# Unpacking 64-bit weights with three bit operations in place of four on VectorE

## The chip, the cores and the metric

The kernel runs on one core of a Trainium2 chip. The metric is the device time of one execution in microseconds. A core has five engines that run side by side, each its own queue in order: TensorE (PE in the profile; PEld is its weight load), VectorE (DVE), ScalarE (ACT), GpSimd (POOL) and SyncE (SP), which here only issues DMAs. They wait for each other by semaphores.

## The reference

Attention with a window and with global tokens (8 batches, 8 heads, 512 local and 32 global tokens, head size 64), and behind it a feed-forward block over the 8 x 544 tokens:

```python
s_ll = scale * np.matmul(q_l, k_l.transpose(0, 1, 3, 2))
mask = np.abs(pos[:, None] - pos[None, :]) <= window
...
x = np.ascontiguousarray(attn_out.transpose(0, 2, 1, 3)).reshape(B * S, H * D)
...
h = x @ w_in
g = np.maximum(h, 0.0) + np.log1p(np.exp(-np.abs(h)))
return (g @ w_out).astype(np.float32)
```

The two weights (512 x 2048 and 2048 x 512) come as 64-bit floats, all else as 32-bit floats.

## The kernel before

**Feed-forward.** Each product is formed from three matmuls in TensorE's rounded 32-bit format: a value is split into a rounded high part and the rest, and high by high, high by rest and rest by high are added. `hpart` makes h for 128 hidden units (f, sixteen of them) and 512 tokens of a batch (b), `act` makes g of it (ScalarE: L529 to L531 and the rounding L535; VectorE: L532, which also frees the bank of h; GpSimd: the rest, L536), `opart` adds g times w_out up. h has two banks, so the third h waits for the first L532. `split_x` and, for the first heads, `split0` split the attention's output into xh (ScalarE) and xl (VectorE, L225).

**Attention.** The first eight heads (four pairs, m below 4) go through a pipeline of steps in `local` and `glob`: `scores0`, maximum and exponentials (`soft0`, L164 to L167), weighing on GpSimd (L179), transposes, products with v. The other head pairs go in pieces: `scores` into s_ps (L306 copies them to SBUF on ScalarE, L311 takes maxima into mt), `maxima` folds them (L324 to L337), `probs` lays them out again with VectorE transposes (L345, tile mb, two buffers), subtracts on GpSimd (L350 to L353), takes exponentials (L354) and sums (L359, tile zt); `totals` inverts the sums; `values` and `normalise` make the output (v_ps, L394 to L399). All pieces of later batches lie among the feed-forward products of the batch before.

**The weights.** A weight tile (kind wi or wo, number k from 0 to 15) is 128 x 512 64-bit floats, which `load_w` brings to SBUF as pairs of 32-bit words, low and high. It becomes 32-bit floats in four bit steps and is then split:

- `abs_w` (L468, ScalarE): absolute value of the high word, read as a 32-bit float, into the tile wbits.
- `bits_w` (VectorE): L475 raises it to at least 2^-15, so that the exponent can't fall out of range; L477 shifts it left by 3 and masks the upper two bits off; L478 puts the high word's upper two bits back in; L481 puts the low word's upper three bits in at the bottom. The result is the 32-bit float, written over the low word.
- `halves_w`: L486 rounds it (ScalarE), L487 takes the rest (GpSimd).

The tiles go in the order of `order_w`: wi0 to wi3, wo0, wo1, wi4, wi5, wo2, wo3, wi6, wi7 and so on. Eleven or twelve of them are handled in the steps of the first heads, one a step, with VectorE's and ScalarE's order there written out by `keep` and `note`; the rest (`weights`) beside batch 0 of the feed-forward block.

**The order.** TensorE's order is written out: `mm` chains every matmul to the one before. On VectorE, ScalarE and GpSimd a list scheduler with a timeline of its own sets the order outside the chained steps, from its own costs of the instructions; so a change of one instruction can move others.

Of the kernel before, what the change touches and what calls it, by code (L numbers as in the profile page):

```python
# [8 lines left out]
F32 = mybir.dt.float32  # L9
# [3 lines left out]
AF = mybir.ActivationFunctionType  # L13
ALU = mybir.AluOpType
# [28 lines left out]
SPACE = 3  # L43
AHEAD = 4

TINY = 2.0 ** -15


def windows(ap2d, start, stride, count, width):
# [5 lines left out]
def moe_over_global_local_attention(  # L55
# [11 lines left out]
    nc = tc.nc  # L67
# [51 lines left out]
    def after(i, what):  # L119

        if what in order:
            tc.add_manual_dep(i.ins, order[what].name, mybir.DependencyInfo(mybir.DependencyClass.NoSync, mybir.DependencyReason.DATA), reason="order")
        return i
# [26 lines left out]
    def keep(what, i):  # L150
        order[what] = after(i, what).ins
# [292 lines left out]
    wi, wo, raws = {}, {}, {}  # L444
# [13 lines left out]
    def note(what, i):  # L458
        if tight:
            keep(what, i)  # L460
        return i

    def abs_w(kind, k):
        if A_LO <= k < NF - A_UP:
            a = pl.tile([P, 512], I32, tag=f"{kind}{k + A_UP}", name=f"wbits{kind}{k}", bufs=1)
        else:
            a = pl.tile([P, 512], I32, tag="mb", name=f"wbits{kind}{k}", bufs=2)
        note("act", nc.scalar.activation(a.bitcast(F32), raws[kind, k][:, :, 1].bitcast(F32), AF.Abs))  # L468
        return a

    def bits_w(kind, k, a):
        t = raws.pop((kind, k))
        lo32, hi32 = t[:, :, 0], t[:, :, 1]

        i = nc.vector.tensor_scalar(a.bitcast(F32), a.bitcast(F32), TINY, None, op0=ALU.max)  # L475
        note("dve", i) if tight else after(i, "maxima")
        note("dve", nc.vector.tensor_scalar(a, a, 3, 0x3FFFFFFF, op0=ALU.logical_shift_left, op1=ALU.bitwise_and))  # L477
        note("dve", nc.vector.scalar_tensor_tensor(a, hi32, -0x40000000, a, op0=ALU.bitwise_and, op1=ALU.bitwise_or))  # L478

        r = lo32 if k < NF - 1 else pl.tile([P, 512], I32, tag="mb", name=f"wlast{kind}", bufs=2)  # L480
        note("dve", nc.vector.scalar_tensor_tensor(r, lo32, 29, a, op0=ALU.logical_shift_right, op1=ALU.bitwise_or))  # L481
        return r.bitcast(F32)
# [6 lines left out]
    def split_w(kind, k):  # L489
        halves_w(kind, k, bits_w(kind, k, abs_w(kind, k)))  # L490
# [104 lines left out]
    i = order_w.index(("wi", NF - 1))  # L595
# [39 lines left out]
    for k in range(-2, n + 2):  # L635
        stage(k + 2, 0)

        while k >= n - 2 and pcs[0][0] < min(12 * M0 + 8 * (k - n + 3), START):
            pcs.pop(0)[1]()
        if k == 0:  # L640
            key_masks()
        if held:
            r = bits_w(*held)
        stage(k + 2, 1)
        stage(k - 2, 5)
        stage(k - 2, 6)
        stage(k, 3)
        stage(k, 4)
        stage(k + 2, 2)
        if held:  # L650
            halves_w(*held[:2], r)
            held = None
        if -1 <= k and wk[1] < W_PRE:
            held = order_w[wk[1]]
            held += (abs_w(*held),)
            wk[1] += 1
    tight = False
    if held:
        halves_w(*held[:2], bits_w(*held))
# [74 lines left out]
```

## Time and profile before

| | us |
|---|---|
| median of three runs | 1016.42 (1015.89 to 1018.9) |
| profiled execution | 1018.0 |
| its span, first to last instruction | 1016.2 |
| TensorE busy | 963.4 |
| VectorE busy | 676.4 |
| ScalarE busy | 512.6 |
| GpSimd busy | 451.7 |

The profile is of one execution. In a line of the 40 slices each digit is the busy share in tenths of a slice of 25 us; PEclk is the clock that TensorE was granted. In a group of instructions stand line, engine, operation, output and inputs with shapes, count, then busy time in all, mean time of one in ns, and the engine's idle time just before them. In a timeline a row has start and length in us. Neighbouring instructions of one engine overlap by some hundredths of a microsecond.

### The profile page before, as it was taken

The page shows a single profiled execution, that of the slowest core. Times are in us where ns is not written, and L with a number is a line of the kernel's source. Part 1 is how long each engine was busy: PE and PEld are TensorE (multiplying, and loading weights), DVE is VectorE, ACT ScalarE, POOL GpSimd, SP SyncE. Part 2 cuts the span into 40 slices and gives each one's busy share as a digit, 9 for nine tenths or more (in the row PEclk, how much of TensorE's full clock was granted, in tenths as well). Part 3 has the DMA queues.
Part 4 walks back from the last instruction along what each step waited for, and adds up shares of the span by engine and source line. Part 5 has one row for each costly group of instructions (what it writes and reads, how often), then busy time and mean ns, then how long its engine had stood idle before and what let it go on. Part 6 is the DMA issues. An engine that isn't in the chain of part 4 may idle for free.

```text
span 1016.2 us, 14213 instructions
## 1 busy us (share of the span) xinstructions
PE 963.4 (95%) x5098; PEld 750.6 (74%) x5098; DVE 676.4 (67%) x1428; ACT 512.6 (50%) x882; POOL 451.7 (44%) x614
## 2 busy tenths in 40 slices
PE   6685988999999999999999999999999999999996
PEld 4553666777777777777777777777777777888895
DVE  6879989797667767776678766776677665211210
ACT  5754655555444544554445544554455445544452
POOL 4645675654444544344444544444435444222221
PEclk9897988999999999999999999999999999999998
DMA  9540441121111211121112111121112100100000
GB/s 353 206 146 19 167 140 57 51 70 53 44 48 48 85 42 46 35 88 48 39 48 89 48 42 43 57 80 44 41 47 76 46 17 1 63 0 1 22 22 21
DMA packets 34607, 65.94 MB, mean 65 GB/s; under 512 B 7656, under 2 KB 11752, under 8 KB 34536
## 3 DMA queue, kind: packets, MB, share of 16 engines
q1 hardware_dynamic: 33992, 64.96, 20.0%
q8 instruction: 40, 0.66, 0.3%
q14 instruction: 31, 0.25, 0.1%
q10 hardware_dynamic: 544, 0.07, 0.0%
HBM read 55.57 MB, written 9.44 MB: 64 GB/s over the span
## 4 chain that ended last, share of the span: by engine, by line
PE 81%; DVE 9%; POOL 3%; issue 3%; ACT 2%; DMA 1%; SPq 0%; POOLq 0%; ACTq 0%; DVEq 0%
PE o L126 35%; PE h L126 34%; PE s_ps L126 6%; PE v_ps L126 5%; POOL s L350 1%; DVE wbitswi L478 1%; DMA woraw<-in_w_out 1%; DVE wiraw L481 1%; DVE sums L164 1%; DVE wbitswo L478 1%; DVE wbitswi L475 1%; POOL gl L536 1%; ACT e L167 1%; POOL wo L487 1%; DVE wbitswo L475 0%
## 5 line engine op out<-in xcount | busy, mean ns | idle before, releaser
L126 PE MATMUL h<-xh,wi 128*128 128x512 f32 (+1 forms) x1152 | 351.7, 389 | 18.6 <-DVE xl L225 12.7
L126 PE MATMUL o<-wo,gh 128*128 128x512 f32 x1088 | 347.2, 400 | 0.0
L536 POOL TENSOR_TENSOR gl<-e,gh 128x512 fp32r<-128x512 f32 x136 | 178.6, 1314 | 328.0 <-ACT gh L535 258.2
L126 PEld LDWEIGHTS h<-xh,wi 128*128 128x128 f32 x1152 | 210.2, 190 | 68.5 <-issue 18.2
L126 PEld LDWEIGHTS o<-wo,gh 128*128 128x128 f32 x1088 | 200.6, 189 | 51.3 <-ACT e L529 3.8
L532 DVE SCALAR_TENSOR_TENSOR e<-h,e 128x512 f32<-128x512 f32 x136 | 93.1, 685 | 218.1 <-ACT e L531 197.2
L126 PE MATMUL h<-xl,wi 128*128 128x512 f32 (+1 forms) x576 | 220.8, 383 | 0.0
L126 PE MATMUL o<-wo,gl 128*128 128x512 f32 x544 | 214.6, 395 | 0.0
L529 ACT ACTIVATE e<-h 128x512 f32<-128x512 f32 x136 | 81.1, 597 | 224.6 <-PE h L126 224.4
L535 ACT CAST gh<-e 128x512 fp32r<-128x512 f32 x136 | 84.3, 620 | 121.3 <-DVE e L532 121.2
L350 POOL TENSOR_TENSOR s<-s,mb 128x384 f32<-128x384 f32 x112 | 114.2, 1049 | 57.4 <-DVE mb L345 57.3
L126 PEld LDWEIGHTS h<-xl,wi 128*128 128x128 f32 x576 | 109.2, 190 | 22.6
L126 PEld LDWEIGHTS o<-wo,gl 128*128 128x128 f32 x544 | 102.7, 189 | 24.0 <-POOL gl L536 0.2
L531 ACT ACTIVATE e<-e,one 128x512 f32<-128x512 f32 x136 | 98.4, 723 | 4.2
L354 ACT ACTIVATE s<-s 128x768 f32<-128x768 f32 (+1 forms) x84 | 66.4, 790 | 47.2 <-POOL s L350 41.7
L530 ACT ACTIVATE e<-e 128x512 f32<-128x512 f32 x136 | 85.7, 630 | 3.3
L310 DVE TENSOR_TENSOR s<-s_ps,mask 128x768 f32<-128x768 f32 (+1 forms) x96 | 64.6, 694 | 29.3 <-PE s_ps L126 29.3
L126 PE MATMUL s_ps<-raw 64*128 64x192 f32 (+1 forms) x672 | 79.0, 348 | 4.5 <-issue 4.5
L126 PEld LDWEIGHTS s_ps<-raw 64*128 64x128 f32 x672 | 53.5, 189 | 36.2 <-issue 28.7
L359 DVE TRANSPOSE_TENSOR_REDUCE zt<-s 128x24 f32<-128x768 f32 (+1 forms) x84 | 75.3, 901 | 6.7 <-ACT s L354 4.5
L311 DVE TRANSPOSE_TENSOR_REDUCE mt<-s 128x24 f32<-128x768 f32 (+1 forms) x84 | 74.6, 888 | 3.6 <-ACT s L306 2.9
L126 PE MATMUL v_ps<-s,v 128*64 128x192 f32 (+1 forms) x672 | 58.1, 324 | 3.9 <-ACT s L306 3.2
(129 smaller groups left out, 852.7 us busy)
## 6 DMA issues: line engine op xcount, KB each, us to landing
raw<-in_qk SPq DMA_DIRECT2D x56, 272.0 KB, 2.7
v<-in_v SPq DMA_DIRECT2D x28, 384.0 KB, 3.0
out<-ot SPq DMA_DIRECT2D x34, 256.0 KB, 2.2
wiraw<-in_w_in SPq DMA_DIRECT2D x16, 512.0 KB, 8.5
woraw<-in_w_out SPq DMA_DIRECT2D x16, 512.0 KB, 7.1
raw<-in_qk SPq DMA_DIRECT2D x28, 224.0 KB, 2.5
v<-in_v SPq DMA_DIRECT2D x4, 512.0 KB, 9.1
raw<-in_qk SPq DMA_DIRECT2D x4, 416.0 KB, 7.4
```

The costliest lines, as they stand in the source:

```text
L126: order["pe"] = after(nc.tensor.matmul(*a, **k), "pe").ins
L310: nc.vector.tensor_tensor(s[:, :, o:o + w], ps[:, :, o:o + w], mk.unsqueeze(1).to_broadcast([P, 2, w]), op=ALU.add)
L311: order["scores"] = nc.vector.tensor_reduce(windows(mt, 3 + 12 * p, 36, 2, nb), s.rearrange("p h (b k) -> p h b k", k=32), axis=AX.X, op=A ...
L350: nc.gpsimd.tensor_tensor(sw, sw, windows(mb[:, h], 0, 96, 2, 192), op=ALU.subtract)
L354: nc.scalar.activation(s, s, AF.Exp, scale=0.125)
L359: nc.vector.tensor_reduce(windows(st["zt", m], 3 + 12 * p, 36, 2, nb), s.rearrange("p h (b k) -> p h b k", k=32), axis=AX.X, op=ALU.add, a ...
L529: nc.scalar.activation(e, ph, AF.Abs)
L530: nc.scalar.activation(e, e, AF.Exp, scale=-1.0)
L531: nc.scalar.activation(e, e, AF.Ln, bias=one)
L532: nc.vector.scalar_tensor_tensor(e, ph, 0.0, e, op0=ALU.max, op1=ALU.add)
L535: nc.scalar.copy(gh, e)
L536: nc.gpsimd.tensor_tensor(gl, e, gh.bitcast(F32), op=ALU.subtract)
```

## The change

```diff
-TINY = 2.0 ** -15
+DROP = 2.0 ** -112
+SIGN = -0x80000000
...
     def abs_w(kind, k):
...
-        note("act", nc.scalar.activation(a.bitcast(F32), raws[kind, k][:, :, 1].bitcast(F32), AF.Abs))
+        note("act", nc.scalar.activation(a.bitcast(F32), raws[kind, k][:, :, 1].bitcast(F32), AF.Copy, scale=DROP))
...
     def bits_w(kind, k, a):
...
-        i = nc.vector.tensor_scalar(a.bitcast(F32), a.bitcast(F32), TINY, None, op0=ALU.max)
+        i = nc.vector.tensor_scalar(a, a, 3, None, op0=ALU.logical_shift_left)
         note("dve", i) if tight else after(i, "maxima")
-        note("dve", nc.vector.tensor_scalar(a, a, 3, 0x3FFFFFFF, op0=ALU.logical_shift_left, op1=ALU.bitwise_and))
-        note("dve", nc.vector.scalar_tensor_tensor(a, hi32, -0x40000000, a, op0=ALU.bitwise_and, op1=ALU.bitwise_or))
+        note("dve", nc.vector.scalar_tensor_tensor(a, hi32, SIGN, a, op0=ALU.bitwise_and, op1=ALU.bitwise_or))
```

ScalarE now multiplies the high word, read as a 32-bit float, by 2^-112. That takes 112 off its exponent field, which holds the upper eight of the 64-bit float's eleven exponent bits, and 112 times 8 is 896, the difference between the two formats' offsets. What is left of the exponent fits below the top when it is shifted left by 3 (new L476), so nothing has to be masked; values too small come out as zero without the maximum. The shift drops the sign, which the merge (new L478) takes from the high word. Per tile VectorE has three instructions (L476, L478, L481) in place of four. The constant's new line moves the line numbers up to L476 by one; from L480 on they are the same.

TensorE has the same instructions in the same order. On VectorE, ScalarE and GpSimd the scheduler moves others, too. Three places matter below. In each the buffer's number is the last part of a name.

VectorE, where the first pair's maxima (mt4) have been folded and head pair 4's transposes (mb4) follow; L311 (new L312) is the reduction of head pair 5's scores. Before:

```order
L337 COPY mt4_656<-mt4_656 32x42 x3
L311 TENSOR_REDUCE mt5_768<-s5_1_816 128x2x12
L345 STREAM_TRANSPOSE mb4_0_739<-mt4_656 128x576
L345 STREAM_TRANSPOSE mb4_1_747<-mt4_656 128x576
L311 TENSOR_REDUCE mt5_768<-s5_2_845 128x2x9
```

and changed:

```order
L338 COPY mt4_648<-mt4_648 32x42 x3
L346 STREAM_TRANSPOSE mb4_0_730<-mt4_648 128x576
L346 STREAM_TRANSPOSE mb4_1_738<-mt4_648 128x576
L312 TENSOR_REDUCE mt5_759<-s5_1_806 128x2x12
L312 TENSOR_REDUCE mt5_759<-s5_2_835 128x2x9
```

The two transposes now stand ahead of the reduction.

VectorE, up to the last xl of the first heads (L225, new L226), the last input of the first feed-forward product. Before:

```order
L337 COPY mt5_768<-mt5_768 32x42 x3
L475 TENSOR_SCALAR wbitswi8_1056<-wbitswi8_1056 128x512
L475 TENSOR_SCALAR wbitswi9_1094<-wbitswi9_1094 128x512
L478 SCALAR_TENSOR_TENSOR wbitswi6_805<-wiraw6_158,wbitswi6_805 128x512
L359 TENSOR_REDUCE zt4_744<-s4_2_723 128x2x9
L345 STREAM_TRANSPOSE mb5_0_861<-mt5_768 128x576
L477 TENSOR_SCALAR wbitswi8_1056<-wbitswi8_1056 128x512
L477 TENSOR_SCALAR wbitswi9_1094<-wbitswi9_1094 128x512
L481 SCALAR_TENSOR_TENSOR wiraw6_158<-wiraw6_158,wbitswi6_805 128x512
L225 TENSOR_TENSOR xl0_3_789<-o0_3_1_885,xh0_3_788 128x256
```

and changed:

```order
L478 SCALAR_TENSOR_TENSOR wbitswi6_795<-wiraw6_158,wbitswi6_795 128x512
L338 COPY mt5_759<-mt5_759 32x42 x3
L476 TENSOR_SCALAR wbitswi8_1042<-wbitswi8_1042 128x512
L476 TENSOR_SCALAR wbitswi9_1079<-wbitswi9_1079 128x512
L360 TENSOR_REDUCE zt4_735<-s4_2_714 128x2x9
L481 SCALAR_TENSOR_TENSOR wiraw6_158<-wiraw6_158,wbitswi6_795 128x512
L226 TENSOR_TENSOR xl0_3_779<-o0_3_1_874,xh0_3_778 128x256
L346 STREAM_TRANSPOSE mb5_0_851<-mt5_759 128x576
```

The shifts of wi8 and wi9 are gone, the transpose of head pair 5 (mb5) stands behind xl, and the first merge of wi6 has moved ahead of the copies. On GpSimd the rest of wi6 (L487) now stands ahead of head pair 5's subtractions, behind the first of which it stood.

ScalarE, where head pair 7's last scores are copied from PSUM (L306, new L307), which frees the bank for the next v_ps. Before:

```order
L486 CAST wo12_1561<-woraw12_1429 128x512
L306 COPY s7_2_1624<-s_ps7_2_1615 128x576
L535 CAST gh0_9_1590<-e0_9_1585 128x512
L486 CAST wo13_1600<-woraw13_1455 128x512
```

and changed:

```order
L486 CAST wo12_1533<-woraw12_1406 128x512
L530 ACTIVATE e0_9_1557<-e0_9_1557 128x512
L531 ACTIVATE e0_9_1557<-e0_9_1557,one_102 128x512
L486 CAST wo13_1571<-woraw13_1431 128x512
L535 CAST gh0_9_1562<-e0_9_1557 128x512
L307 COPY s7_2_1595<-s_ps7_2_1586 128x576
```

The copy now stands behind the rounding of wo13 and of the ninth tile of g (gh0_9), and so behind what VectorE does for them.

## The prediction

> **What bounds the kernel now.** I read the page first, for which engine sets the end and from when on.
>
> ```profile
> span 1016.2 us, 14213 instructions
> PE 963.4 (95%) x5098; PEld 750.6 (74%) x5098; DVE 676.4 (67%) x1428; ACT 512.6 (50%) x882; POOL 451.7 (44%) x614
> PE   6685988999999999999999999999999999999996
> DVE  6879989797667767776678766776677665211210
> PEclk9897988999999999999999999999999999999998
> PE 81%; DVE 9%; POOL 3%; issue 3%; ACT 2%; DMA 1%; SPq 0%; POOLq 0%; ACTq 0%; DVEq 0%
> ```
>
> TensorE (PE) is full except in the first slices of 25 us, where VectorE (DVE) is. The weights are unpacked only there. The stages of the busy-time table make it sharp (in each row: stretch, its length, then busy time of PE, PEld, DVE, ACT, POOL, then the granted clock).
>
> ```profile
> core 0: us, PE busy (x) PEld busy (x) DVE busy (x) ACT busy (x) POOL busy (x), PEclk, DMA share, GB/s
> 14.00:44.00 30.00, 19.63 (x185) 14.83 (x183) 28.93 (x55) 23.28 (x70) 17.73 (x28) 1.00 0.85 327
> 71.00:85.00 14.00, 1.31 (x7) 1.04 (x6) 11.94 (x26) 5.46 (x9) 9.87 (x16) 0.64 0.31 117
> 98.00:110.00 12.00, 12.00 (x51) 8.74 (x52) 11.91 (x24) 7.71 (x13) 9.20 (x6) 0.86 0.45 157
> 110.00:130.00 20.00, 17.84 (x87) 12.78 (x86) 18.14 (x24) 13.28 (x24) 11.69 (x10) 1.00 0.46 162
> 130.00:150.00 20.00, 16.90 (x81) 12.40 (x80) 18.44 (x36) 11.62 (x19) 14.29 (x17) 0.83 0.39 135
> 150.00:170.00 20.00, 18.53 (x92) 13.69 (x90) 19.60 (x32) 10.39 (x18) 11.97 (x10) 1.00 0.09 25
> 170.00:190.00 20.00, 18.71 (x88) 14.52 (x89) 17.18 (x36) 12.14 (x20) 15.61 (x19) 0.83 0.19 63
> 235.00:1000.00 765.00, 765.00 (x4000) 603.45 (x3999) 474.22 (x1033) 373.39 (x601) 316.29 (x435) 1.00 0.15 45
> ```
>
> From 235 us TensorE is busy 765.00 of 765 us at full clock: nothing done on VectorE there can shorten or lengthen the end. Since the order on TensorE is the same in the changed program, the end comes earlier by just as much as TensorE gets through its first 216 us earlier. From 98 to 190 us VectorE is busy 85.3 of 92 us (the five rows summed), while TensorE waits now and then. Its eight longest waits from its first feed-forward product on, from TensorE's timeline (start, length, and in brackets the idle time before it and what ended it):
>
> ```profile
> 84.30 1.19 PE L126 MATMUL h<-xh,wi 128*128 128x512 f32 x2 [12.69 <-DVE xl L225]
> 97.98 0.74 PE L126 MATMUL h<-xh,wi 128*128 128x512 f32 x2 [3.07 <-DVE e L532]
> 114.93 0.73 PE L126 MATMUL h<-xh,wi 128*128 128x512 f32 x2 [0.89 <-DVE e L532]
> 122.03 0.73 PE L126 MATMUL h<-xh,wi 128*128 128x512 f32 x2 [1.27 <-DVE e L532]
> 140.14 1.01 PE L126 MATMUL s_ps<-raw 64*128 64x192 f32 x4 [2.67 <-issue]
> 171.29 3.79 PE L126 MATMUL v_ps<-s,v 128*64 128x192 f32 x24 [2.76 <-ACT s L306]
> 206.39 2.01 PE L126 MATMUL v_ps<-s,v 128*64 128x192 f32 x24 [0.68 <-DVE s L310]
> 214.61 1.47 PE L126 MATMUL s_ps<-raw 64*128 64x192 f32 x8 [1.82 <-issue]
> ```
>
> The sum is 25.85 us, half of it in the first. That is the room.
>
> **The change, part by part.** Per weight tile (32 of them) one VectorE instruction goes. The maximum (old L475) becomes a shift on the same tile, the old shift-with-mask (L477) is gone, and both merges stay.
>
> ```profile
> L477 DVE TENSOR_SCALAR wbitswo<-wbitswo 128x512 int32<-128x512 int32 x16 | 11.6, 730 | 0.3
> L477 DVE TENSOR_SCALAR wbitswi<-wbitswi 128x512 int32<-128x512 int32 x16 | 9.6, 602 | 0.2
> L475 DVE TENSOR_SCALAR wbitswi<-wbitswi x16: 378/424/1512, 15.4 to 185.8; 128x512 f32<-128x512 f32 x16
> L477 DVE TENSOR_SCALAR wbitswo<-wbitswo x16: 407/428/1547, 35.4 to 203.6; 128x512 int32<-128x512 int32 x16
> ```
>
> The new shift is an integer instruction of one operation, of which the trace has none; its neighbours, the float maximum (median 424 ns) and the integer shift-with-mask (428), cost the same, so I count the swap as nothing. The removed one costs 0.43 us by its median, 0.66 by its mean (21.2 us over 32), at least 0.38 (the maximum's least). Median and mean differ by waits for GpSimd (POOL), as one step of the first loop shows:
>
> ```profile
> 20.16 0.55 DVE L477 TENSOR_SCALAR wbitswi<-wbitswi 128x512 int32<-128x512 int32 x1
> 20.40 1.46 POOL L487 TENSOR_TENSOR wi<-wiraw,wi 128x512 fp32r<-128x512 f32 x1
> 20.74 1.66 DVE L478 SCALAR_TENSOR_TENSOR wbitswi<-wiraw,wbitswi 128x512 int32<-128x512 int32 x1
> 23.80 0.66 ACT L468 ACTIVATE wbitswi<-wiraw 128x512 f32<-128x512 f32 x1
> 24.56 0.62 DVE L475 TENSOR_SCALAR wbitswi<-wbitswi 128x512 f32<-128x512 f32 x1
> ```
>
> The merge L478 ends at 22.40, half a microsecond after GpSimd's subtraction ended at 21.86, and took 1.66. Had the shift not stood ahead of it, it or the next merge would have met that subtraction all the same. So I take 0.43, with 0.66 as the upper end. The Trainium skill's page "SBUF — State Buffer" (the section with "The single rule") says the same of a VectorE instruction with two SBUF inputs against a GpSimd instruction that reads SBUF: the second to start blocks for the whole of the first. By that rule the waits pass on to the merges, and counting the mean would be wrong; the rows of this step agree.
>
> On ScalarE the absolute value becomes a copy with a scale. A copy with a scale at this shape is not in the trace; an exponential with a scale is, and the copies of the page lie beside it:
>
> ```profile
> L530 ACT ACTIVATE e<-e 128x512 f32<-128x512 f32 x136 | 85.7, 630 | 3.3
> ```
>
> 630 ns against the absolute value's 660: I take no difference. Should it cost more, that is a rival below.
>
> *Stage A, 0 to 44 us.* The loop over the first heads is VectorE's: 28.93 of 30 us. Six tiles (wi0 to wi3, wo0, wo1) stand ahead of the last scores' maximum in it. In a step the removed instruction takes 0.58 from its start to the next start (20.16 to 20.74). Six by 0.5, between the two prices: 3.0 us (bounds 6 by 0.38 = 2.3 and 6 by 0.66 = 4.0). Tiles wi4 and wi5 lie beside a TensorE chain: nothing.
>
> *Stage B, 44 to 84 us,* which ends with the 12.69 us wait. Rows of VectorE:
>
> ```profile
> 69.42 0.98 DVE L311 TRANSPOSE_TENSOR_REDUCE mt<-s 128x24 f32<-128x768 f32 x1
> 70.33 1.40 DVE L345 STREAM_TRANSPOSE mb<-mt 128x576 f32<-128x576 f32 x2
> 80.99 0.74 DVE L345 STREAM_TRANSPOSE mb<-mt 128x576 f32<-128x576 f32 x1
> 81.65 0.77 DVE L477 TENSOR_SCALAR wbitswi<-wbitswi 128x512 int32<-128x512 int32 x2
> 82.34 1.48 DVE L481 SCALAR_TENSOR_TENSOR wiraw<-wiraw,wbitswi 128x512 int32<-128x512 int32 x1
> 83.75 0.41 DVE L225 TENSOR_TENSOR xl<-o,xh 128x256 fp32r<-128x256 f32 x1
> ```
>
> and the spread of the second merge over all its tiles (least, median, longest, ns):
>
> ```profile
> L481 DVE SCALAR_TENSOR_TENSOR wiraw<-wiraw,wbitswi x15: 645/695/1675, 17.4 to 163.7; 128x512 int32<-128x512 int32 x15
> ```
>
> Two tiles (wo2, wo3) lose 0.43 each ahead of the fold: 0.8. The reduction at 69.42 moves behind the two transposes for which GpSimd waits: 0.9 (69.42 to 70.33). Ahead of the last xl, the transpose at 80.99 moves behind it (0.7), the shifts of wi8 and wi9 (0.77) and of wi6 (0.43) are gone: 1.9. The merge L481 took 1.48 where 0.69 is usual, beside GpSimd's subtraction for head pair 5, which now starts later; I count half of the 0.8 back: 0.4. Sum of B: 4.0 (bounds 2.6, with no reordering gain on GpSimd's side and no wait given back, and 5.0). So the first product would come 7.0 us earlier, at about 77.3.
>
> *Stage C, 84 to 216 us.* Sixteen more tiles stand ahead of the wait at 171.29: 16 by 0.43 = 6.9 us of VectorE's queue. Against that: the transpose that left stage B now lies between the first product and the first L532, where one shift is gone (net 0.3 lost, so the 3.07 us wait stays). And on ScalarE the copy that ends the wait at 171.29 now stands behind the rounding of wo13 and of the ninth g tile: two ScalarE instructions (2 by 0.63, as the rows near it) and, on VectorE, two merges of wo13 less its shift (2 by 0.69 - 0.43 = 0.95). Together 2.2, of which I take 1.7, since a part lies side by side. 6.9 - 0.3 - 1.7 = 4.9. The waits for it to come out of (0.89, 1.27, 2.67, 2.76) hold 7.6. Parts of these waits are ScalarE's own queue, which loses nothing, so I take 4.0. The last three tiles (wi15, wo14, wo15) wait for a load that follows TensorE's own progress: nothing. Bounds: 0 (everything meets another wait) and 19 by 0.66 = 12.5.
>
> The clock: 0.83 in both stages with a gap of 2.7 us, so each costs some 0.17 by 20 = 3.4 us of TensorE. Since I leave gaps of one to two microseconds, and the one of 1.82 shows no more than that gaps of this size occur, I count no window saved; upper end two, 6.8. The Trainium skill's page "TensorE: Matmul & The Clock Gate" (Part 1) has the clock halved after about 3.4 us idle; by that, gaps of 2.7 would cost nothing and shortening them only their own length, so the sum stays. This trace differs: both such gaps lie in rows with 0.83.
>
> **Sum.** 3.0 + 4.0 + 4.0 = 11.0 us off a span of 1016.2: 1005.2. The profiled execution took 1018.0, 1.8 around its span, and the median of the runs is 1016.42, 1.6 below it. So 1005.4 for the median.
>
> **Rivals.**
> - *The waits for GpSimd go too, and with them gaps and half-clock windows.* For it: the means of 602 and 730 against medians near 430. Against: the step at 20 us. A 4.0 + B 5.0 + C 7.6 and one window of 3.4: 20 off, 996.4.
> - *Only the start moves.* VectorE was not what held 140 and 171 us: "issue" and ScalarE stand there as releasers. For it: ScalarE's copy moved backward. Against: VectorE's 93% in these stages. 7 off, 1009.4.
> - *Nothing moves.* The loop turns on GpSimd or the loads (DMA share 0.85 in stage A). Against: VectorE has 1 us idle in 30 there. About 1015.5.
> - *Slower: the scaled copy is dearer on ScalarE.* In a loop step the scaling ends at 24.46 and the shift starts at 24.56, so all it takes beyond 0.1 us more delays each of six steps, then wi6, then about half of C's 19 tiles: 6 + 1 + 9.5 = 16.5 times the excess. It decides from an excess of 0.7 us (660 to 1360 ns), where the 11 us are eaten; at 1.0, 5.5 slower, 1021.9. The exponential with a scale at 630 ns speaks against it.
>
> **How the numbers follow.** Forecast 0.52; waits go too 0.16; only the start 0.21; nothing 0.06; slower 0.05. What a measurement of this kernel can tell from no change is about 0.3%, or 3 us. Faster is the first three: 0.89; same 0.06; slower 0.05. The range reaches into both neighbours: from 18 off to 5.4 off (A 2.3, B 2.6 and half a microsecond of C), 998 to 1011.
>
> **What would show it.** L477 gone, VectorE's instructions 32 fewer, the merges' mean up rather than down if waits pass on. The first product near 77 with a wait of 8 to 10 us. The wait at 98 unchanged, seen from the first product; those at 115 and 122 nearly gone; that at 171 shorter by a microsecond or two. L468 near 660 ns. The forecast is wrong in its first step if the scaling that starts at 23.80 now starts later than 23.3 (two shifts, 1.0 us, are gone by then), and in its third if TensorE's idle time between its first product and 216 us falls by less than 2 or by more than 8.

## The result: 8 to 10 us faster

The changed kernel takes 1008.58 us in the median (1008.38 to 1008.7) against 1016.53 for the kernel before on the same chip, a ratio of 0.9912 with a 95% interval of 0.9898 to 0.9926. Measured again later it was 0.9900 (0.9885 to 0.9914). The forecast, 1005.4, is a ratio of 0.9892; the time lies inside the range, two to three microseconds above the forecast.

The page of the profile after, its head and the slices of TensorE, VectorE and the granted clock:

```profile
span 1006.8 us, 14177 instructions
PE 959.9 (95%) x5098; PEld 747.8 (74%) x5098; DVE 663.4 (66%) x1396; ACT 513.8 (51%) x882; POOL 452.0 (45%) x614
...
PE   6776989999999999999999999999999999999996
...
DVE  6879897886777766776668677776677665211210
...
PEclk9887989999999999999999999999999999999999
```

VectorE has 32 instructions fewer and 13.0 us less busy time, 0.41 us each. The span is 9.4 us shorter. The stages, with the columns of the table of before:

```profile
14.00:44.00 30.00, 21.67 (x187) 15.95 (x185) 28.06 (x51) 25.08 (x76) 20.60 (x31) 0.93 0.83 319
71.00:85.00 14.00, 6.87 (x28) 5.06 (x30) 12.97 (x27) 5.05 (x8) 10.26 (x15) 0.54 0.20 78
98.00:110.00 12.00, 11.79 (x60) 8.65 (x56) 11.91 (x15) 6.31 (x12) 8.11 (x7) 1.00 0.50 168
110.00:130.00 20.00, 17.90 (x97) 13.60 (x98) 14.55 (x22) 13.56 (x24) 13.66 (x12) 1.00 0.52 180
130.00:150.00 20.00, 16.89 (x72) 11.99 (x71) 19.80 (x36) 13.08 (x21) 16.16 (x16) 0.83 0.32 110
150.00:170.00 20.00, 18.61 (x105) 14.47 (x104) 15.85 (x30) 11.06 (x19) 10.95 (x11) 1.00 0.24 72
170.00:190.00 20.00, 19.28 (x92) 15.01 (x91) 18.02 (x34) 10.75 (x17) 13.69 (x15) 1.00 0.17 46
```

VectorE is still nearly full in the first loop (28.06 of 30 us), from 98 to 110 us (11.91 of 12) and from 130 to 150 us (19.80 of 20). From 110 to 130 us, where it had 18.14 of 20, it has 14.55, and from 150 to 170 us, where it had 19.60, it has 15.85: in these two stretches it now waits too. The clock of 170 to 190 us is 1.00 where it was 0.83. TensorE's waits from its first feed-forward product on:

```profile
78.13 1.19 PE L127 MATMUL h<-xh,wi 128*128 128x512 f32 x2 [8.14 <-DVE xl L226]
...
93.75 0.82 PE L127 MATMUL h<-xh,wi 128*128 128x512 f32 x2 [3.95 <-DVE e L532]
110.87 0.72 PE L127 MATMUL h<-xh,wi 128*128 128x512 f32 x2 [1.08 <-DVE e L532]
117.92 0.72 PE L127 MATMUL h<-xh,wi 128*128 128x512 f32 x2 [1.23 <-DVE e L532]
135.98 1.01 PE L127 MATMUL s_ps<-raw 64*128 64x192 f32 x4 [3.11 <-issue]
165.62 2.01 PE L127 MATMUL v_ps<-s,v 128*64 128x192 f32 x24 [1.39 <-ACT s L307]
...
198.53 2.01 PE L127 MATMUL v_ps<-s,v 128*64 128x192 f32 x24 [0.54 <-DVE s L311]
206.28 0.92 PE L127 MATMUL s_ps<-raw 64*128 64x192 f32 x8 [1.35 <-issue]
```

Row by row against before, the same product starts 6.17 us earlier (84.30 to 78.13), then 4.23, 4.06, 4.11, 4.16, 5.67 (171.29 to 165.62), 7.86 (206.39 to 198.53) and 8.33 (214.61 to 206.28). So after the first product nearly 2 us of the gain are lost by 94 us, and most of them come back only near 165 us; 3.7 us of the 9.4 come behind that. One row of busy time over the same 652 matmuls in both shows what became of it; first before, from its first product to 235 us, then after, to 225.60 (235 less the 9.4 us of the span):

```profile
84.30:235.00 150.70, 136.46 (x652) 102.61 (x653) 133.86 (x250) 87.17 (x147) 90.44 (x94) 0.92 0.26 87
```

```profile
78.13:225.60 147.47, 132.81 (x652) 99.75 (x652) 128.69 (x232) 87.48 (x147) 91.53 (x95) 0.95 0.27 89
```

The start gives 6.17 us. Behind it the stretch is 3.23 shorter: TensorE's idle time (length less busy) went from 14.24 to 14.66, no less at all, and the same matmuls took 3.65 less busy time, since less of it ran at half clock. Whether that is a cause or only where the time shows up is what the experiments had to tell.

### The profile page after: what moved, and what is told of

The parts are those of the page before. It is cut to its first block, busy times and chain, and to the rows that moved or that the text cites. A ratio compares the mean times of both kernels' runs of the same rounds, so it can differ in the third digit from the quotient of the medians.

```text
span 1006.8 us, 14177 instructions
## 1 busy us (share of the span) xinstructions
PE 959.9 (95%) x5098; PEld 747.8 (74%) x5098; DVE 663.4 (66%) x1396; ACT 513.8 (51%) x882; POOL 452.0 (45%) x614
## 4 chain that ended last, share of the span: by engine, by line
PE 82%; DVE 9%; ACT 3%; POOL 3%; issue 3%; DMA 0%; POOLq 0%; ACTq 0%; DVEq 0%
PE h L127 35%; PE o L127 35%; PE s_ps L127 6%; PE v_ps L127 5%; POOL s L351 1%; DVE wbitswi L478 1%; ACT e L168 1%; DVE wiraw L481 1%; POOL gl L536 1%; DVE sums L165 1%; POOL wo L487 1%; DVE wbitswo L478 1%; DVE wbitswi L476 1%; PE s0g L127 0%; DVE mb L346 0%
## 5 line engine op out<-in xcount | busy, mean ns | idle before, releaser
L532 DVE SCALAR_TENSOR_TENSOR e<-h,e 128x512 f32<-128x512 f32 x136 | 93.1, 684 | 221.6 <-ACT e L531 200.7
L311 DVE TENSOR_TENSOR s<-s_ps,mask 128x768 f32<-128x768 f32 (+1 forms) x96 | 64.6, 694 | 28.3 <-PE s_ps L127 28.3
L312 DVE TRANSPOSE_TENSOR_REDUCE mt<-s 128x24 f32<-128x768 f32 (+1 forms) x84 | 74.6, 889 | 5.1 <-ACT s L307 4.3
L127 PEld LDWEIGHTS v_ps<-s,v 128*64 128x64 f32 x672 | 46.1, 137 | 17.6 <-issue 9.3
```

What stands on the lines that cost most here:

```text
L127: order["pe"] = after(nc.tensor.matmul(*a, **k), "pe").ins
L311: nc.vector.tensor_tensor(s[:, :, o:o + w], ps[:, :, o:o + w], mk.unsqueeze(1).to_broadcast([P, 2, w]), op=ALU.add)
L312: order["scores"] = nc.vector.tensor_reduce(windows(mt, 3 + 12 * p, 36, 2, nb), s.rearrange("p h (b k) -> p h b k", k=32), axis=AX.X, op=A ...
L532: nc.vector.scalar_tensor_tensor(e, ph, 0.0, e, op0=ALU.max, op1=ALU.add)
```

## The experiments

The main theory: VectorE's queue up to about 165 us sets the end, and each instruction less in it counts, wherever it stands. The rivals: something else in the change (the scaled copy, the kind of instruction, what the scheduler moved); only the start moves; the gain behind the start is half-clock windows that happened not to fall.

**The count alone.** The shift by 3 in two steps: VectorE has four instructions a tile again, and the order of every engine is word for word that of before.

```diff
-        i = nc.vector.tensor_scalar(a, a, 3, None, op0=ALU.logical_shift_left)
+        i = nc.vector.tensor_scalar(a, a, 1, None, op0=ALU.logical_shift_left)
         note("dve", i) if tight else after(i, "maxima")
+        note("dve", nc.vector.tensor_scalar(a, a, 2, None, op0=ALU.logical_shift_left))
```

> The changed kernel with its shift by 3 split into a shift by 1 and a shift by 2, so VectorE has four instructions a tile again (1428 in all) and every engine's order is the one of before; only the kinds of two of the four and ScalarE's scaled copy differ. Theory (the number of VectorE instructions a tile is what counts; a scaled copy costs ScalarE what the absolute value cost, an integer shift what the maximum cost): 1016.5, between 1015 and 1018, first product at 84.3 +- 0.5, L469 near 660 ns. Rival (part of the gain comes from the scaled copy or from the kind of the instructions): below 1014.

Measured: ratio 0.9993 (0.9984 to 1.0002), first product at 85.03, 0.2 us later than the forecast allowed (two profiles of one kernel, below, differ by 0.85 there). The gain is gone. ScalarE's scaled copy, the integer shift in place of the maximum and the changed merge are together worth nothing that could be measured. In the changed kernel the scaled copy took this (least, median, longest, ns), where the absolute value had taken 0.66 us:

```profile
L469 ACT ACTIVATE wbitswi<-wiraw x16: 645/671/696, 13.7 to 175.3; 128x512 f32<-128x512 f32 x16
L469 ACT ACTIVATE wbitswo<-woraw x16: 648/668/702, 32.5 to 190.7; 128x512 f32<-128x512 f32 x16
```

**Early tiles, late tiles.** The second shift only for the twelve tiles of the first heads' steps (so only the late twenty gain), and only for the other twenty.

```diff
-        i = nc.vector.tensor_scalar(a, a, 3, None, op0=ALU.logical_shift_left)
+        i = nc.vector.tensor_scalar(a, a, 1 if tight else 3, None, op0=ALU.logical_shift_left)
         note("dve", i) if tight else after(i, "maxima")
+        if tight:
+            note("dve", nc.vector.tensor_scalar(a, a, 2, None, op0=ALU.logical_shift_left))
```

(the other kernel has `not tight` in both places)

> The twelve tiles of the first heads' steps keep four VectorE instructions (two shifts), the other twenty have three. Theory (an instruction less shortens VectorE's queue in either part): the first product stays at 83.5 to 84.3, and 1 to 4 us come off behind it: 1012.5 to 1015.5. Rival 'only the start moves': 1016.5 +- 1. Rival 'clock' (the changed kernel's gain behind the first product was half-clock windows not met, which depends on where a gap falls, not on these twenty instructions): anywhere between 1012 and 1018, with the number of half-clock windows between 98 and 235 us (three before, one after) going with it, 1.7 or 3.4 us each.

> The reverse: the twelve tiles of the first steps have three VectorE instructions, the other twenty four (two shifts). Theory: the first product at 78.1 + 0.8 (two late tiles' extra shifts lie ahead of it) = 78.9, and the end at 1008.6 + 1 to 4 = 1010 to 1012.5. Rival 'only the start moves': 1008.6 to 1009.4. Rival 'it is all in the late tiles': above 1014.

Measured: the late tiles alone 0.9952 (0.9937 to 0.9967), first product at 84.22; the early ones alone 0.9962 (0.9948 to 0.9976), first product at 78.31. The product of the two is 0.9914, the change's own 0.9912 and 0.9900. So "only the start moves" falls: twenty tiles that leave the first product where it was bring about half, and those that bring the first product 6 us forward bring 3.9 us (0.0038 of 1018) at the end. On the scale of before at 1016.5 the late kernel is 1011.6, faster than the theory's 1012.5 to 1015.5, and the early one 1012.6, just beyond the slow end of its 1010 to 1012.5: of its 6 us at the first product, over 2 were lost again behind it.

**One instruction less again.** The shift left out as well.

```diff
-        i = nc.vector.tensor_scalar(a, a, 3, None, op0=ALU.logical_shift_left)
-        note("dve", i) if tight else after(i, "maxima")
-        note("dve", nc.vector.scalar_tensor_tensor(a, hi32, SIGN, a, op0=ALU.bitwise_and, op1=ALU.bitwise_or))
+        i = nc.vector.scalar_tensor_tensor(a, hi32, SIGN, a, op0=ALU.bitwise_and, op1=ALU.bitwise_or)
+        note("dve", i) if tight else after(i, "maxima")
```

> The changed kernel without its shift (the exponent stays where the scaling left it, so the weights have other values): two VectorE instructions a tile, 1364 in all. Theory (VectorE's queue still sets the start and most waits up to 135 us): the first product another 4 to 6 us earlier, 72 to 74, and the end at 1001 to 1004. Rival (waits for GpSimd and ScalarE's chain take over): first product not before 76, end at 1006 to 1008.6.

Measured: 0.9814 (0.9801 to 0.9828), first product at 71.50. The second instruction is worth as much as the first, 0.0086 to 0.0098 of the time or 9 to 10 us, and the end at 998 on the scale of before at 1016.5 lies beyond the theory's own 1001 to 1004. (The weights have other values here, so the kernel stands for its time alone.) In the first loop ScalarE (26.43 of 30 us) has come level with VectorE (26.23).

**What the scheduler moved.** The changed kernel with the orders of VectorE, ScalarE and GpSimd pinned to those of before, by a table of the instructions' names.

```diff
     assert not pcs
+    made = {i.name: i for i in nc.cur_bb.bb.instructions}
+    for names in OLD_ORDER:
+        for x, y in zip(names, names[1:]):
+            tc.add_manual_dep(made[f"I-{y}"], f"I-{x}", mybir.DependencyInfo(mybir.DependencyClass.NoSync, mybir.DependencyReason.DATA), reason="order")
```

> The changed kernel with the order of VectorE, ScalarE and GpSimd held to that of before (only L477 is gone from it). Theory (the gain is the VectorE time of 32 instructions; what the scheduler moved is worth nothing in itself): within 1 us of the changed kernel, ratio 0.989 to 0.9925 to before, first product 78 to 79. Rival (the reordering that the prediction counted in its second stage, 0.9 + 0.7 us, and ScalarE's copy that moved backward behind two roundings, 1.7 us lost later, are real): first product at 79.7 and the wait near 165 us gone or shorter, 1007 to 1010 in all, so it is the first product that tells.

Measured: 0.9886 (0.9871 to 0.9901), first product at 81.23. The reordering does bring the first product forward, by 3.1 us (81.23 against 78.13), and the end has nothing of it: the old order is, if anything, 1 to 3 us faster than the changed kernel, with intervals that overlap. The part of the forecast on ScalarE's copy was wrong: TensorE's wait for it, 1.39 us in the changed kernel, is 3.02 here, longer and not gone. It is the fastest kernel of this study that computes all, by a margin that these runs don't settle.

This kernel and the one with two shifts have the same order on all three engines, the one of before, and the same scaled copy and merge. They differ alone in the shift being one instruction or two, 32 instructions in all: 0.9993 against 0.9886, 11 us. That is the cleanest measure of what the count is worth.

**Moving the waits.** Three more orders. In the first the two merges that stood ahead of head pair 5's normalisation go behind it (the dependency on the normalisation's third product is added for both); in the second the steps of the first heads take ten tiles instead of twelve, which puts the last xl ahead of 14 instructions; in the third both.

```diff
+        if m == 5:
+            order["norm"] = i
+            tc.add_manual_dep(merges[-1], i.name, mybir.DependencyInfo(mybir.DependencyClass.NoSync, mybir.DependencyReason.DATA), reason="order")
```

```diff
-W_PRE = 12
+W_PRE = 10
...
-    loads(W_PRE + 2)
+    loads(14)
...
-    loads(W_PRE + 6)
+    loads(18)
```

> The changed kernel with two merges (L478 of the two wo tiles that stood ahead of head pair 5's normalisation L395 to L397) ordered behind it on VectorE. In the changed kernel's profile these two merges took 2.46 us beside GpSimd's subtractions, L397 ended at 135.88 and TensorE's wait of 3.11 us at 135.98. Theory (VectorE's order ends that wait, and a gap of this size draws a half-clock window of 6.8 us, 3.4 us of work): the gap falls to 0.5 to 1.0 us, no half-clock window between 130 and 145 us, the end 2.3 + 3.4 = 5.7 us earlier, 1003; 1006.3 if only the gap goes. Rival (the wait, told as 'issue', has another cause, a load or ScalarE): gap 2.5 or more, 1008.6.

> The changed kernel with ten weight tiles in the first heads' steps instead of twelve (wi6 and wi7 go to the later ones), loads as they were. VectorE's order then has the last xl, for which TensorE waited 8.14 us at 78.13, ahead of 14 instructions that stood before it, and the first L532 ahead of 24. Theory (the start is set by VectorE's and ScalarE's order, not by a load): first product at 70 to 71.5, a wait of at most 2 us; of the 7 to 8 us so won at least half stays behind (the instructions moved come later, in a full queue): 1001 to 1004.5. Rival (all VectorE work ahead of 130 us has to be done anyway, so the wait only moves to the L532's): 1007 to 1009, with waits for L532 of 8 us or more in place of 6.3.

> Both edits together. If they are independent, the sum of the two gains over the changed kernel's 1008.6: about 997 by the first theories of both.

Measured: 0.9923 (0.9907 to 0.994), 0.9908 (0.9893 to 0.9923) and 0.9929 (0.9914 to 0.9943): none better than the changed kernel, against forecasts of 4 to 11 us. Each did what it says. With the merges behind, TensorE's wait of 3.11 us is 0.70 and the half-clock window there is gone; but a wait of 4.89 stands near 165 us where 1.39 was:

```profile
133.19 0.59 PE L127 MATMUL s_ps<-raw 64*128 64x192 f32 x4 [0.70 <-PE o L127]
...
167.71 3.79 PE L127 MATMUL v_ps<-s,v 128*64 128x192 f32 x24 [4.89 <-ACT s L308]
```

With the last xl ahead, the first product starts at 70.49 without a wait, 7.6 us earlier; 25 us later stands this:

```profile
95.77 1.01 PE L127 MATMUL s_ps<-raw 64*128 64x192 f32 x4 [12.19 <-issue]
```

On VectorE's timeline of that kernel L397, the last instruction of the first normalisation that reads v_ps, whose bank these scores take, ends at 95.66: the instructions that xl was moved past come between. The rival had the time right and the place wrong: the wait stands at these scores, not at the L532's. In all three kernels an order decided only at which product TensorE waited. The reading is that VectorE's work has to be done by some later product all the same; it is argued from these places, for VectorE is not busy throughout. From 14 us to the product near 165 it is idle 18.59 us in the changed kernel (to 165.62) and 12.78 in the one before (to 171.29).

**The changed kernel once more.** Unaltered, as a second profile.

> The changed kernel unaltered, a second profile on the same chip as the others. Theory on the clock (it is decided on a grid of 3.41 us periods that runs free of the program; a period in which TensorE is idle 2.0 us or more is followed by half clock, 1.8 or less is not): the same gaps within 0.2 us, but the half-clock windows fall elsewhere, and a gap of 1.3 to 3.1 us may now draw one or not, by where the grid cuts it. Rival (a gap of a certain length draws one): the same windows at the same gaps as in the first profile. Time 1008.6 +- 1.5 on the scale of before at 1016.5.

Measured: 0.9900 (0.9885 to 0.9914). The gaps are the same within 0.2 us, but for one at 86 us (1.41 where 1.02 was) and that near 165 us (2.51 where 1.39 was), the first product is at 77.28 instead of 78.13, and the half-clock windows are others. The same matmuls:

```profile
77.28:224.80 147.52, 131.24 (x652) 99.26 (x653) 128.74 (x232) 87.27 (x147) 91.50 (x95) 0.96 0.27 89
```

They took 1.57 us less busy time than in the first profile, because less of it was at half clock, and the stretch is as long, 147.52 against 147.47: TensorE waited 1.62 us more. The kernel with two shifts says the same of before: 132.38 us of busy time instead of 136.46, and a length of 150.97 instead of 150.70. So the 3.65 us that the comparison above put down to the clock are bookkeeping. Two stretches between products with v show it over more kernels. From the one near 130 us to the one near 171, before, two shifts and three in early tiles only take 40.19, 40.21 and 40.21 us, with 7.6, none and 3.4 us of half clock in it; the change takes 39.13 and 39.14 in its two profiles, with 6.8 and 3.4. Behind it, to the second next product with v (171.29 to 237.14 in before), the same three take 65.85, 66.08 and 64.94 us, with 9.4, 6.8 and 3.4 us of half clock; the change takes 62.13 and 62.16 with none, the change with the last xl ahead 62.14 with 3.4, and no shift 59.86 with none. The lengths go with the number of VectorE's instructions and not with the clock. Where VectorE sets the pace, half clock takes time that TensorE would otherwise wait.

**VectorE's work given to ScalarE.** ScalarE also multiplies the high word by zero, which was to leave its sign; VectorE then needs two instructions, in the late tiles only, or in all.

```diff
+        if not tight:
+            hi = raws[kind, k][:, :, 1].bitcast(F32)
+            note("act", nc.scalar.activation(hi, hi, AF.Copy, bias=-0.0, scale=0.0))
+            two.add((kind, k))
...
+        if (kind, k) in two:
+            i = nc.vector.scalar_tensor_tensor(a, a, 3, hi32, op0=ALU.logical_shift_left, op1=ALU.bitwise_or)
+            note("dve", i) if tight else after(i, "maxima")
```

(the other kernel has `True` for `not tight`)

> The changed kernel, but for the twenty later tiles ScalarE also multiplies the high word by 0 (with a bias of -0), in place, which leaves its sign alone, and VectorE needs two instructions: a merge of the scaled word shifted by 3 with that sign, and the second merge. VectorE has 1376 instructions, ScalarE 902. Theory (what is taken off VectorE's queue ahead of 165 us comes off the end; ScalarE, 10 to 13 of 20 us busy there, has room): 20/32 of the 9 us that no_shift's shift was worth: 5 to 6 us under the changed kernel, 1002.5 to 1003.5 on the scale of before at 1016.5. Rival (ScalarE's twenty instructions more, 13 us, lie in the chain that ends TensorE's wait near 165 us, which was put down to ScalarE's copy L307): no gain or slower, 1008 to 1013.

> The same for all 32 tiles: VectorE 1364 instructions as in no_shift, ScalarE 914. Theory (room on ScalarE everywhere): as no_shift, ratio 0.9814, 998 on the scale of before at 1016.5. Rival (in the first heads' steps ScalarE is 25.08 of 30 us busy and six more instructions of 0.67 fill it: the steps then turn on ScalarE, and the first product comes no earlier than 78): 1002.5 to 1006, no better than two_late.

The weights that these two make are not the meant ones (what ScalarE's product by zero leaves was not looked into), so they stand for their times alone: 0.9903 (0.9887 to 0.9919) and 0.9904 (0.9883 to 0.9924), nothing gained on the changed kernel. VectorE has as few instructions in the second as without the shift, and without the shift the end was 9 us earlier. In the first loop ScalarE took VectorE's place as the full engine, as the rival said (28.60 of 30 us, VectorE 22.96):

```profile
14.00:44.00 30.00, 20.59 (x192) 15.54 (x190) 22.96 (x45) 28.60 (x79) 18.76 (x31) 1.00 0.84 323
```

The rival's other sign, a first product not before 78, came out at 77.21. In the late tiles ScalarE has room by its busy time, and a gain was there for a while: the product with v that starts at 198.53 in the changed kernel starts at 195.51 with the late tiles and at 194.99 with all. The lead shrinks to 1.8 and 1.9 us at the next scores, which wait 1.35 us in the changed kernel and longer here, and to 0.7 and 0.9 by the product with v at 227.75. First the kernel with the late tiles, then that with all:

```profile
204.51 0.92 PE L127 MATMUL s_ps<-raw 64*128 64x192 f32 x8 [2.60 <-issue]
```

```profile
204.37 1.05 PE L127 MATMUL s_ps<-raw 64*128 64x192 f32 x8 [2.98 <-issue]
```

In each of the three, VectorE's L397 ends 0.10 us before these scores start. So part of what was won was given back at another wait for VectorE. Why VectorE, with less to do, is not earlier there stays open. A weight passes ScalarE, VectorE, ScalarE and GpSimd in turn, so an instruction handed from one engine to the next lengthens that chain; that this is the reason is argued, not shown.

**GpSimd's share.** The rest of each weight (L487) is not computed but set to zero, with a shorter GpSimd instruction.

```diff
-        nc.gpsimd.tensor_tensor(o[:, 1], r, o[:, 0].bitcast(F32), op=ALU.subtract)
+        nc.gpsimd.memset(o[:, 1].bitcast(F32), 0.0)
```

> The changed kernel with GpSimd's subtraction L487 (the rest of each weight, 44.6 us in 30 instructions) left out and the rest set to zero instead, so the weights are the rounded ones alone. In the changed kernel the three VectorE instructions of a tile take 78.5 us in 32 tiles; at the usual 0.43 + 0.69 + 0.69 us they would take 58: 20 us are waits for GpSimd, for L487 and for the scores' subtractions L351. Theory (VectorE's time ahead of 165 us sets the end, waits included): L478 and L481 fall towards 690 ns, some half of the 20 us goes, and about two thirds of that comes off the end: 1001 to 1004. Rival (the waits pass on to GpSimd's other instructions, or ScalarE's chain holds the end as in two_late): 1006 to 1008.6.

Measured: 0.9781 (0.9765 to 0.9797), 12 to 13 us under the changed kernel, about twice what the theory had. The merges did get shorter, first in the changed kernel, then without the rests:

```profile
L478 DVE SCALAR_TENSOR_TENSOR wbitswi<-wiraw,wbitswi 128x512 int32<-128x512 int32 x16 | 14.9, 934 | 0.2
L481 DVE SCALAR_TENSOR_TENSOR woraw<-woraw,wbitswo 128x512 int32<-128x512 int32 x15 | 15.0, 1002 | 0.1
```

```profile
L478 DVE SCALAR_TENSOR_TENSOR wbitswi<-wiraw,wbitswi 128x512 int32<-128x512 int32 x16 | 12.2, 768 | 0.3
L481 DVE SCALAR_TENSOR_TENSOR woraw<-woraw,wbitswo 128x512 int32<-128x512 int32 x15 | 11.4, 767 | 0.1
```

All merges together fall from 57.5 to 48.3 us, 9 us, and the end by more: GpSimd also has 32 instructions of 0.53 us in place of 32 subtractions of about 1.5 us ahead of its other work. How much each has of it was not separated. VectorE's busy time as a whole falls by 14.7 us (663.4 to 648.7) and the span by 13.2, about the rate at which removed instructions came off. So for this kernel GpSimd's rests cost more than a bit operation of all tiles, 12 to 13 us against 9 to 10.

The same matmuls behind the first product (652; two profiles have one record less), from the busy-time rows of the profiles. The end is 235.0 us in the kernel before and, in the others, earlier or later by the difference of the spans. Idle is length less TensorE's busy time. The last column is VectorE's busy time in the whole profile, its waits inside instructions included:

| kernel | first product | length | busy | idle | end | VectorE busy |
|---|---|---|---|---|---|---|
| before | 84.30 | 150.70 | 136.46 | 14.24 | 235.0 | 676.4 |
| two shifts | 85.03 | 150.97 | 132.38 | 18.59 | 236.0 | 676.4 |
| three in early tiles only | 78.31 | 152.99 | 136.22 | 16.77 | 231.3 | 671.9 |
| three in late tiles only | 84.22 | 144.28 | 131.74 | 12.54 | 228.5 | 668.7 |
| the change | 78.13 | 147.47 | 132.81 | 14.66 | 225.6 | 663.4 |
| the change, again | 77.28 | 147.52 | 131.24 | 16.28 | 224.8 | 663.4 |
| the change, old order | 81.23 | 142.67 | 130.65 | 12.02 | 223.9 | 662.5 |
| no shift | 71.50 | 143.00 | 131.01 | 11.99 | 214.5 | 650.4 |
| no rests | 75.10 | 137.30 | 128.33 | 8.97 | 212.4 | 648.7 |
| two in late tiles, ScalarE one more | 78.45 | 146.45 | 132.98 | 13.47 | 224.9 | 657.3 |
| two in all tiles, ScalarE one more | 77.21 | 147.49 | 133.92 | 13.57 | 224.7 | 647.5 |

The start and the length trade against each other. In the first nine rows the end goes with the work on VectorE, 0.7 to 0.85 us for each microsecond that comes off it. The last two rows break the rule: VectorE has least to do in the last, and the end is that of the change. So VectorE's busy time decides as long as nothing is added to its neighbours in the chain of a weight. Whether it is VectorE's queue as such or the length of that chain which a removed instruction shortens, these runs don't separate, since a removed instruction shortens both.

## Why the forecast came out as it did

**What bounds the kernel** was right: full TensorE from 235 us on (755.00 of 755 us up to 990 in the changed kernel too), and VectorE ahead of it. Removing VectorE's time, and nothing else in the change, moved the end.

**The price of an instruction**, 0.43 us by its median and not 0.66 by its mean, was near enough: 13.0 us of VectorE's busy time over 32 is 0.41. (The 428 ns are the median of the wo tiles; that of the wi tiles is 495.) In the unpacking alone it is 0.50: its instructions took 94.5 us and take 78.5. The waits for GpSimd passed on to the merges, as the step at 20 us had suggested: the mean of a merge rose from 848 to 898 ns, the sign that the prediction had set. In the same step of the changed kernel the first merge stands where the removed shift stood, and takes what it took in before; in the step behind it, as in the next two, it is now the second merge that takes this long:

```profile
19.50 0.55 DVE L476 TENSOR_SCALAR wbitswi<-wbitswi 128x512 int32<-128x512 int32 x1 [0.41 <-ACT wbitswi L469]
20.08 1.66 DVE L478 SCALAR_TENSOR_TENSOR wbitswi<-wiraw,wbitswi 128x512 int32<-128x512 int32 x1
...
24.56 0.82 DVE L478 SCALAR_TENSOR_TENSOR wbitswi<-wiraw,wbitswi 128x512 int32<-128x512 int32 x1
25.41 1.67 DVE L481 SCALAR_TENSOR_TENSOR wiraw<-wiraw,wbitswi 128x512 int32<-128x512 int32 x1
```

**ScalarE's scaled copy** costs what the absolute value cost (671 and 668 ns), and the swap of the maximum for a shift costs nothing: both as forecast, and shown together by the kernel with two shifts. That values too small come out as zero, as the text on the change has it, no run here shows.

**Stage A, 3.0 us forecast, 2.2 measured.** The last reduction of the loop starts at 41.38 after and at 43.58 before, just under the lower bound of 2.3. The step that failed: "so many tiles by the price", with nothing new in the way. The rows show it: VectorE now waits 0.41 us for ScalarE's scaling in the step at 19.50, and 0.17 us for ScalarE's exponentials at 40.77, which it didn't before. The last reduction of the loop, first before, then after:

```profile
43.58 1.08 DVE L164 TENSOR_REDUCE sums<-s 128x4 f32<-128x896 f32 x1
```

```profile
41.38 1.08 DVE L165 TENSOR_REDUCE sums<-s 128x4 f32<-128x896 f32 x1
```

The scaling that had to start by 23.3 for the step to stand starts at 23.13.

**Stage B, 4.0 us forecast, 4.0 measured** (6.17 at the first product less 2.2). The sum was right by luck, since two parts missed by as much each way. The reordering, which I had put at 2.0, is worth 3.1 by the old order (81.23 against 78.13, one profile each). So 0.9 is left for the removed instructions, where I had counted 2.0. The two tiles ahead of the fold, 0.8 of it, brought nothing there: the first fold (L327, new L328) starts at 66.85 before and at 64.91 after, 1.94 earlier, less than the 2.2 of stage A. VectorE waits longer for ScalarE's scaling ahead of them, first before, then after:

```profile
62.36 1.05 DVE L475 TENSOR_SCALAR wbitswo<-wbitswo 128x512 f32<-128x512 f32 x1 [1.77 <-ACT wbitswo L468]
```

```profile
60.75 1.05 DVE L476 TENSOR_SCALAR wbitswo<-wbitswo 128x512 int32<-128x512 int32 x1 [2.68 <-ACT wbitswo L469]
```

Wrong was also the use made of the reordering: I added it to the end, and pinned to the old order the kernel ends no later.

**Stage C, 4.0 us forecast, 3.2 measured in the profile** (1.8 to 4 by the medians, 8 to 10 less 6.2), by another way than I said. The waits at 115 and 122 were to be nearly gone; they are 1.08 and 1.23, as before. The wait at 98 grew from 3.07 to 3.95. On VectorE, between the first product and the L532 that ends this wait, two merges now stand beside GpSimd's subtractions and take 3.14 us where 1.38 is usual; that they are what made it longer is argued, not shown:

```profile
78.59 3.14 DVE L478 SCALAR_TENSOR_TENSOR wbitswi<-wiraw,wbitswi 128x512 int32<-128x512 int32 x2
```

That at 171 shrank as forecast in the first profile, from 2.76 to 1.39, but is 2.51 in the second, so this says little. By the condition that the prediction set (TensorE's idle time from its first product on falls by 2 to 8 us) its third step was wrong: it went from 14.24 to 14.66. I had summed the gain over TensorE's waits as if each were its own; the runs show that a wait shortened in one place comes back in another, and that the end follows VectorE's total work. Nor does it stop at 165 us, as the main theory had it: 3.7 of the 9.4 us come behind.

**The clock.** "No window saved" was wrong as a reading of the profile (the windows near 171 and 215 us are gone). It was harmless for the time, since the stretches above are as long with half clock as without. Likewise the upper end, which counted 3.4 us for a window, would have been wrong.

**The rivals.** "Only the start moves" had 0.21 and gave 1009.4, closer to the first measured median than my own forecast (the later ratio, 0.9900 or 1006.3, is closer to the forecast); its mechanism is refuted by the late tiles' 0.9952. "The waits for GpSimd go too" didn't come about, and the last experiment shows what GpSimd's part is worth, its work and its waits together: 12 us, where I had put 9 between that rival and my forecast. The slower rival, a dearer scaled copy, is off: 671 ns.

## What to carry to other kernels

Ahead of a full engine, ask which engine's total work has to be done by then, and price a change by the time it takes off that engine (here some 0.8 us at the end for each microsecond of VectorE); a sum over the waits of the waiting engine counts the same gain in several places. An earlier start or a shorter wait that comes from reordering alone is given back at a later product: four reorderings here, one of them 7.6 us earlier at the first product, brought nothing. Before taking work off an engine by giving it to its neighbour in the same chain, see whether the neighbour or the chain has room; 32 instructions moved from VectorE to ScalarE were worth nothing, 32 removed were worth 9 us.

## What the hardware showed that I had not expected

**The clock is granted in periods of 3.41 us** that lie differently against the program in each execution. All stretches of half clock in the fourteen profiles are one to four such periods long, but for the last in each, which the end of the program cuts. First the changed kernel around its 3.11 us wait, by periods, then its second profile around the same wait:

```profile
131.80:135.22 3.42, 1.07 (x5) 0.55 (x3) 3.42 (x5) 0.75 (x2) 3.19 (x3) 1.00 0.00 0
135.22:138.63 3.41, 2.65 (x13) 1.49 (x13) 3.41 (x7) 2.73 (x6) 3.41 (x3) 0.50 0.00 0
138.63:142.04 3.41, 3.41 (x10) 2.67 (x9) 3.41 (x6) 3.07 (x6) 3.41 (x6) 0.50 0.35 82
```

```profile
130.02:133.43 3.41, 1.97 (x9) 1.28 (x7) 3.41 (x6) 0.00 (x0) 2.29 (x2) 1.00 0.05 20
133.43:136.84 3.41, 1.74 (x13) 1.15 (x14) 3.41 (x6) 2.57 (x5) 3.41 (x4) 1.00 0.00 0
136.84:140.26 3.42, 3.42 (x9) 2.65 (x8) 3.42 (x7) 3.06 (x6) 3.42 (x5) 0.50 0.12 13
```

In the first, 2.35 us of the wait lie in one period: the next is at half clock, and as TensorE is idle 0.76 us in that one too, a second follows. In the second profile the same wait is cut into 1.44 and 1.67: one period of half clock instead of two. In the kernel with two shifts a wait of 2.68 us was cut into 1.26 and 1.41, and no half clock followed at all. Among the periods that start from 85 to 232 us in all fourteen profiles, one at full clock with 1.66 us of idle time or less was never followed by half clock (523 of them), one with 2.0 or more always (23); between 1.67 and 1.94 both occur. At half clock, a period with at most 0.46 us idle was the last in all but two cases of 34, and one with 0.47 or more was always followed by another.

The Trainium skill's page "TensorE: Matmul & The Clock Gate" (Part 1) has a free-running window of about 3.4 us and half clock after at least one idle window. The free-running window is what these traces show; "idle" here means from about 1.7 to 2.0 us of the 3.41 on, so a wait of 2.7 us can draw half clock or not, by where it falls. My prediction took the trace's 2.7 us gaps as a length that draws a window; it is a matter of how a period cuts them.
